# Two query-weight blocks kept in place of half a V tile, and the query block expanded by VectorE

## The chip, the core and the metric

One Trainium2 chip; the program runs on one core. The metric is device time in microseconds of one execution. The kernel before has a median of 177.51 us in three runs (177.19 to 177.63).

## What is computed

One token per sequence, four sequences, passes through two equal layers. Each layer adds attention over a cache (32 query heads, 8 key/value heads of 128, the last 2048 positions) and then a gated feed-forward block, each behind a normalisation.

```python
q = (x @ wq).reshape(B, Sq, Hq, Dh)            # x: 4 x 512, wq: 512 x 4096
k, v = k_cache[:, :, Sk - W:, :], v_cache[:, :, Sk - W:, :]
scores = einsum("bhqd,bhkd->bhqk", q, k) * Dh ** -0.5
o = einsum("bhqk,bhkd->bhqd", softmax(scores), v)
A(x) = o.reshape(B, Sq, Hq * Dh) @ wo
B(x) = (sigmoid(x @ w_gate) * (x @ w_up)) @ w_down
x = x + A(layernorm(x)); x = x + B(layernorm(x))   # twice, with the same weights and caches
```

## The kernel before

Nearly everything it does is stream weights and caches from HBM once per layer through 50 SBUF slots of 512 KB (`arena`) and one more buffer (`side`). K (16 MB) is read once and stays for both layers, transposed in place by VectorE (`k_transpose`, L887). V is read in both layers, except for what stays from the first to the second: tiles (7,1) and (6,1), tile (7,0), which is packed into PSUM in between, and half of tile (6,0). All these loads are issued by SyncE, in one fixed order, one call to `dma` (L401) each. A load waits until the slot it goes to has been released, and every load behind it waits too. `load` takes a slot pair from a pool in order of release; `load_half` names the half pair it will go to (`homes`), so its place and its releaser are written by hand.

The order of the instructions on each compute engine is made by a planner (`_schedule`) that runs when the program is built, from durations written down in the kernel. While the second layer is planned, `P.chain` fixes TensorE's order to that of the source; VectorE, ScalarE and GpSimdE are ordered by the planner.

The parts that the change touches:

- **Query weights of the second layer** (`load_wq`, L522 to 530; `q_mms`, L817; `q_second`, L857). wq is 512 x 4096, cut into four row blocks c of 128, each in two column halves i. Half i = 1 serves heads 4 to 7, which are attended first in the second layer (heads run 7 to 0). The piece (0,1) stays from the first layer (`keep_wq`, L632). Seven pieces of 512 KB are read again, in the order (1,1), (2,1), (3,1), (0,0), (1,0), (2,0), (3,0), where (c,i) names the row block and the half.
- **Half a V tile** (`keep_half`, L626; `load_v`, L609). The second half of V tile (6,0) stays, so the second layer reads only one half of that tile.
- **The query block** (`q_unit`, L867). For each head, four matmuls with a shifted window of a wide identity (L875) write a block-diagonal 128 x 256 query block into PSUM, and ScalarE copies it to SBUF (L880).
- **The score mask** (`e_m`, L902). Four matmuls of 32 output rows each (L905) put a large negative number into a score bank, before the sixteen score matmuls (L916) add to it.
- **The normalisation between feed-forward and second attention** (`layer_norm`, L743; end of `glu`, L1453). VectorE adds the feed-forward result to x (L1455), sums x (L754), TensorE sums over partitions (L759), and only then the query matmuls can start.

One head of attention in the second layer is called a unit here. In steady state, TensorE does per unit: value matmuls of this unit (L1088), a permutation of the next unit's probabilities (L957), the mask and scores of a unit three ahead (L905, L916), sums (L1064), the query block of the unit after that (L875), and an output projection (L1142). VectorE does: the row maximum of the scores (L929), a reciprocal (L1066), two half copies (L933), a masked maximum (L937, L941), a transposition and reduction of the value result (L1097, L1102, L1104), and the transposition of the probabilities (L964) for which the next value matmuls wait.

Of the kernel before, what the change touches and what calls it, by code (L numbers as in the profile page):

```python
# [7 lines left out]
BF16 = mybir.dt.bfloat16  # L8
ACTF = mybir.ActivationFunctionType
ALU = mybir.AluOpType  # L10
# [268 lines left out]
def build(nc, A_x, A_k, A_v, A_wq, A_wo, B_wg, B_wu, B_wd, out, cfg=None):  # L279
# [45 lines left out]
    with es:  # L325
        def sb(name, shape, dt):
            return es.enter_context(nc.sbuf_tensor(name, shape, dt))
# [10 lines left out]
        eyew = sb("eyew", [128, 224], BF16)  # L338
# [4 lines left out]
        msk_s = sb("msk_s", [128, 32], BF16)  # L343
# [76 lines left out]
        on_free = {}  # L420
        Y = ("V", HKV - 1, 0, 0)
        Z = ("V", HKV - 1, 1, 0)
        GA = ("V", HKV - 2, 0, 0)
        KEPT = ("kept",)
        WQ = ("wq", 0, 0)
        SP = ("side",)
# [11 lines left out]
        def take_load():  # L438
            take_k()
            assert can_take()  # L440
            name, emit = loads.pop(0)
            if name in homes:
                hfree.difference_update(home(name))
                s = home(name)[0]
            else:
                s = pool.alloc()
            where[name] = s
            if name in (Y, Z, GA, WQ):
                base[name] = s
            emit(s)  # L450
# [71 lines left out]
        def load_wq(k):  # L522
            if k == 0:
                for c in range(NC):
                    load(("wq", c, k), 2, "bw_8k", (2 * SLOT, wq_d[:, c, :], False))
            else:
                for i in (1, 0):
                    for c in range(i, NC):
                        load_half(("wq", c, k, i), wq_d[:, c, i * SLOT:(i + 1) * SLOT], "bw_4k", SLOT,
                                  (((Y, 0), (Y, 1), (WQ, 1), (WQ, 0)), (None, (WQ, 0), (GA, 0), (SP, 0)))[i][c])  # L530

# [22 lines left out]
        def load_glu(k):  # L554
            for nm, src, two in (("wg", wg_d, wg_p), ("wu", wu_d, wu_p)):
                if k == 0:
                    for c in range(NC):
                        load_half((nm, c, k), src[:, c, :], "bw_3k", F,
                                  (((WQ, 0), (GA, 0), (SP, 0), (Y, 0)), ((Y, 1), (Z, 0), (WQ, 0), (GA, 0)))[nm == "wu"][c])
                    continue  # L560
                for cc in range(NC // 2):
                    load((nm, cc, k), 2, "bw_8k", (2 * F, two[:, cc, :], False))
            for n, (a, b) in enumerate(bounds_of(k)):
                if k == 0:
                    load_half(("wd", a, k), wd_d[:, a:b, :].rearrange("p k n -> p (k n)"), "bw_4k", (b - a) * D,
                              ((SP, 0), (Y, 0), (Y, 1), (Z, 0))[n])
                else:
                    load(("wd", a, k), 1, "bw_8k", ((b - a) * D, wd_d[:, a:b, :], False))
# [40 lines left out]
        def load_v(h, bp, k, n_use):  # L609
            name = ("V", h, bp, k)  # L610
            tiles = {(HKV - 2, 0): ((GA, 0),), (HKV - 3, 1): ((Y, 0), (Y, 1))}.get((h, bp)) if k else None
            if tiles is not None:
                halves[h, bp] = []
                for n, tile in enumerate(tiles):
                    half = ("Vh", n, h, bp, k)
                    load_half(half, pair_d(A_v, h, bp)[:, :, n * SLOT:(n + 1) * SLOT], "bw_4k", SLOT, tile)
                    halves[h, bp].append((half, 0))
                if len(tiles) == 1:
                    halves[h, bp].append((KEPT, 0))
                return  # L620
            load(name, n_use, "bw_8k", (2 * SLOT, pair_d(A_v, h, bp), True))
# [4 lines left out]
        def keep_half(s):  # L626
            hfree.add(s)
            where[KEPT] = s + 1
            left[KEPT] = 2
        on_free[GA] = keep_half  # L630

        def keep_wq(s):  # L632
            hfree.add(s)
            name = ("wq", 0, 1, 1)
            where[name] = s + 1
            left[name] = 1
            on_free[name] = lambda s: hfree.add(s)
        on_free[WQ] = keep_wq

# [7 lines left out]
        P.op("gpsimd", "eyew0", 200.0, lambda g: g.memset(eyew[:], 0.0), w=[("eyew0",)])  # L647
# [4 lines left out]
        for jh in range(2):  # L652
            for bp in range(2):
                for i in range(2):
# [10 lines left out]
             lambda g: g.affine_select(msk_s[:, :].rearrange("p (i y) -> p i y", i=2),  # L665
                                       ones_f[:, :].rearrange("p (i y) -> p i y", i=2),
                                       [[1, 2], [0, NR]], ALU.is_equal, 0.0, base=-1, channel_multiplier=1),
# [15 lines left out]
             lambda v: v.tensor_reduce(eyew[:, 96:128], ident.rearrange("p (a j) -> p j a", a=4), AXX, ALU.max),  # L683
             r=[("e", 0), ("eyew0",)], w=[("eyew",)])
# [6 lines left out]
        ey = eyew[:, 96:128]  # L691
# [11 lines left out]
        P.op("vector", "selw", 100.0, lambda v: v.tensor_copy(selw[:, :], eyew[:, 96:96 + NB]), r=[("eyew",)], w=[("selw",)])  # L703
# [39 lines left out]
        def layer_norm(tag, b0, b1, for_q, add=None):  # L743
# [12 lines left out]
            if after is not None:  # L756
                after()
            P.op("tensor", "ln_sum" + tag, tm["pe_f32"],
                 lambda t: t.matmul(mean, ones_d, lnr[:, 0:nb], start=True, stop=True),  # L759
# [97 lines left out]
        def q_second(variance):  # L857
            q_mms(1, 1, WB, (0, 1))
            variance()
            unstash_half(tuple(named("ln_rd2Q")))  # L860
            q_mms(1, 1, WB, (2, 3))
            q_mms(1, 0, OBS[1], (0,))
            fresh.append(q_turn(1, 1, WB))
# [3 lines left out]
        def q_unit(tag, h, k2):  # L867
            hh = h % 4
            src = qh[32 * hh:32 * hh + 32, h // 4 * 64:h // 4 * 64 + 64].rearrange("p (x r) -> p x r", r=REP)
            dst = ps[:, CB, 0:256].rearrange("p (x y) -> p x y", y=NR)  # L870

            def e_qx(pe):
                last = None
                for a in range(4):
                    last = pe.matmul(dst[:, :, a * REP:(a + 1) * REP], eyew[32 * hh:32 * hh + 32, 96 - 32 * a:224 - 32 * a],  # L875
                                     src, start=True, stop=True)
                return last
            P.op("tensor", "qx" + tag, 250.0, e_qx, r=[("qh", h // 4), ("eyew",)], w=[("cb",)], banks=(CB,))
            P.op("scalar", "qe" + tag, c_act(256),
                 lambda a: a.copy(qbd[:, k2 * 256:(k2 + 1) * 256], ps[:, CB, 0:256]),  # L880
                 r=[("cb",)], w=[("q", k2)], banks=(CB,))
# [12 lines left out]
        def softmax_unit(tag, hk, wait=False, q=True, between=None):  # L894
# [7 lines left out]
            def e_m(pe):  # L902
                last = None
                for gi in range(4):
                    last = pe.matmul(ps[32 * gi:32 * gi + 32, bank, :], msk_s[:, :],  # L905
                                     msk_m[:, :].unsqueeze(1).broadcast_to([128, 256, 2]), start=True, stop=False)
                return last

            def e_s(pe):
                last = None if wait else e_m(pe)  # L910
                for cp in range(4):
                    for gi in range(4):
                        jh, bp = gi // 2, gi % 2
                        kt = kpair(hk, bp).rearrange("p (j c k t) -> p c t j k", c=2, k=32, t=2)
                        q0 = ((k2 * 4 + cp) * 2 + bp) * 32
                        last = pe.matmul(ps[32 * gi:32 * gi + 32, bank, :], qbd[:, q0:q0 + 32],  # L916
                                         kt[:, cp // 2, cp % 2, jh * NJ:(jh + 1) * NJ, :], start=False, stop=(cp == 3))
                return last
# [74 lines left out]
        def pv_unit(tag, h, k2, tiles, between=None):  # L993
            ob = OBS[k2]
            ev = ebuf[:, k2 * 256:(k2 + 1) * 256].bitcast(BF16).rearrange("p (m x t) -> p t m x", x=32, t=2)
            for n, (bp, name) in enumerate(tiles):
                if n and between is not None:
                    between()
                s = need(name)

                def e_pv(pe, s=s, bp=bp):
                    last = None
                    src = tile_ap(s)
                    for j in range(2 * NJ):
                        x0 = j // 16 * 16 + bp * 8
                        last = pe.matmul(ps[:, ob, bp * 8:bp * 8 + 8], src[:, j * 128:(j + 1) * 128],  # L1006
# [3 lines left out]
                     r=tok(s) + [("e", k2)], w=[("pso", k2, bp)], banks=(ob,))  # L1010
                done(name)
# [224 lines left out]
        def attn_second():  # L1236
# [33 lines left out]
            score(0, lambda: q_mms(1, 0, OBS[1], (1,)))  # L1270
            qx(1)
# [68 lines left out]
        def glu(k, b0, b1, add=None, last=False):  # L1340
# [29 lines left out]
            for n, nm in enumerate(("wg", "wu")):  # L1370
# [21 lines left out]
                if n == 0:  # L1392
# [11 lines left out]
                         lambda v: v.reciprocal(eg[:, 0:NH], eg[:, 0:NH]), r=[("eg",)], w=[("eg",)])  # L1404
            P.op("vector", "gh%d" % k, c_dve(NH),
# [30 lines left out]
            for (a, b) in bounds_of(k):  # L1436
# [3 lines left out]
                def e_d(pe, a=a, b=b, s=s):  # L1440
                    last = None
                    src = slot_ap(s)
                    for fc in range(a, b):
                        for c in range(NC):
# [8 lines left out]
            xts = [("xT", b) for b in range(b0, b1)]  # L1453
            P.op("vector", "gres%d" % k, tm["dve_fix"] + 40.0,
                 lambda v: v.tensor_tensor(bview(xT[:, 0:NX], b0, b1),  # L1455
                                           ps[:, CB, 128:128 + NC * nb].rearrange("p (c b) -> p c b", b=nb),
                                           bview(xT[:, 0:NX], b0, b1), ALU.add),
# [42 lines left out]
        q_second(layer_norm("Q", 0, NB, True))  # L1500
# [73 lines left out]
```

## Time and profile before

The profile is of one execution, which took 177.0 us; 175.3 us of it is the span from the first to the last instruction.

| | before |
|---|---|
| median of three runs | 177.51 us |
| profiled execution, span | 177.0 us, 175.3 us |
| read from HBM | 69.73 MB, mean 398 GB/s over the span |
| busy: TensorE, VectorE, ScalarE, GpSimdE | 105.7, 104.4, 32.7, 22.2 us |
| granted TensorE clock, mean | 0.949 |
| chain that ended last, by engine | DMA 52%, VectorE 24%, TensorE 19% |

How to read it: PE is TensorE's matmul row and PEld its weight loads, DVE is VectorE, ACT ScalarE, POOL GpSimdE, SP SyncE. A row such as `L929 DVE TENSOR_REDUCE small<-ps 128x1 f32<-128x512 f32 x16` names source line, engine, operation, the tile written and the tile read, shapes, and how many there were. In a timeline the first column is the start in us from the span's start, the second how long; square brackets tell how long the engine was idle before it and what ended that. A table by stages gives for each engine the busy time and the number of instructions, then granted clock, busy share of the DMA engines, and GB/s.

### The profile page before, as it was taken

Reading aid. Unit: us, or ns where it says so; the run is one execution under the profiler, and the core shown is the slowest. Engines: PE = TensorE matmul, PEld = TensorE weight load, DVE = VectorE, ACT = ScalarE, POOL = GpSimd, SP = SyncE. Lnnn points to the kernel's source line nnn. Section 1 sums busy time; section 2 is a strip of 40 time slices with the busy share of each in tenths; the row PEclk is TensorE's granted clock in tenths of the full one; section 3 lists DMA queues with packets and bytes.
Section 4 is the critical chain, followed back from the end, with each engine's and each line's share of the span. In section 5 each row is a group of like instructions: output and inputs, shape, how many; then the busy total and the mean of one; then the engine's idle time right before and its main releaser. Section 6 shows DMA issues by size and latency. Waiting matters only on the chain.

```text
span 175.3 us, 3927 instructions
## 1 busy us (share of the span) xinstructions
PE 105.7 (60%) x1661; PEld 54.7 (31%) x1661; DVE 104.4 (60%) x257; ACT 32.7 (19%) x87; POOL 22.2 (13%) x90
## 2 busy tenths in 40 slices
PE   0536246259566273661765456547977999776673
PEld 0203112014334041340445452142322444445321
DVE  6307997994957738378322381316299999751351
ACT  2002031322303003021030000100143455430011
POOL 6100010101101001010010000000011453442000
PEclk9999999999999999999999999999999999995555
DMA  5999999999999999999999999999999999999980
GB/s 188 426 426 426 426 419 424 408 421 423 419 419 412 420 424 426 421 405 427 419 419 415 415 400 407 402 410 403 394 413 404 423 419 424 421 416 423 419 344 25
DMA packets 12226, 70.00 MB, mean 399 GB/s; under 512 B 1320, under 2 KB 1328, under 8 KB 6064
## 3 DMA queue, kind: packets, MB, share of 16 engines
q1 hardware_dynamic: 12200, 69.74, 97.1%
q8 instruction: 13, 0.21, 0.5%
q14 instruction: 5, 0.04, 0.1%
q10 hardware_dynamic: 8, 0.00, 0.0%
HBM read 69.73 MB, written 0.00 MB: 398 GB/s over the span
## 4 chain that ended last, share of the span: by engine, by line
DMA 52%; DVE 24%; PE 19%; issue 2%; SPq 1%; ACT 0%; DVEq 0%
DMA arena<-in_A_v_cache_dram 20%; DMA arena<-in_B_w_down_dram 18%; DVE arena L887 12%; DMA arena<-in_A_wq_dram 10%; PE ps L916 8%; DMA arena<-in_B_w_gate_dram 5%; DVE small L929 3%; PE ps L905 3%; PE ps L1088 2%; DVE small L933 1%; DVE arena L593 1%; PE ps L1006 1%; DVE side L937 1%; PE ps L828 1%; DVE small L941 1%
## 5 line engine op out<-in xcount | busy, mean ns | idle before, releaser
L887 DVE STREAM_TRANSPOSE arena<-arena 128x1024 f32<-128x1024 f32 x32 | 37.0, 1205 | 0.1
L1006 PE MATMUL ps<-side,arena 128*128 128x8 bf16 x576 | 18.2, 168 | 14.1 <-DMA arena<-in_A_v_cache_dram 14.0
L916 PE MATMUL ps<-arena,side 128*32 128x512 bf16 x256 | 25.0, 524 | 0.1
L1006 PEld LDWEIGHTS ps<-side,arena 128*128 128x128 bf16 x576 | 16.7, 104 | 20.5 <-DMA arena<-in_A_v_cache_dram 18.8
L929 DVE TENSOR_REDUCE small<-ps 128x1 f32<-128x512 f32 x16 | 10.8, 676 | 17.6 <-PE ps L916 17.5
L944 ACT ACTIVATE side<-ps,small 128x512 bf16<-128x512 f32 x16 | 11.0, 687 | 36.8 <-PE ps L1024 18.3
L905 PE MATMUL ps<-small,msk_s 128*32 128x512 bf16 x64 | 8.4, 512 | 13.9 <-DVE arena L887 13.1
L880 ACT CAST side<-ps 128x256 bf16<-128x256 f32 x16 | 5.9, 370 | 34.4 <-PE ps L916 25.4
L959 ACT CAST side<-ps 128x512 bf16<-128x512 f32 x16 | 9.4, 586 | 10.8 <-PE ps L957 10.8
L916 PEld LDWEIGHTS ps<-arena,side 128*32 128x32 bf16 x256 | 8.2, 119 | 10.0 <-issue 7.2
L973 POOL CAST small<-small 128x1 bf16<-128x1 f32 x9 | 1.7, 188 | 76.1 <-ACT side L944 76.1
L957 PE MATMUL ps<-side,perm 128*128 128x512 bf16 x16 | 7.9, 494 | 5.2 <-ACT side L944 5.2
L828 PE MATMUL ps<-arena,xn 128*4 128x512 bf16 x60 | 7.5, 572 | 3.9 <-DMA arena<-in_A_wq_dram 3.6
L784 ACT ACTIVATE small<-ps 128x4 f32<-128x4 f32 x4 | 0.7, 174 | 48.1 <-PE ps L780 48.1
L1379 PE MATMUL ps<-arena,xn 128*4 128x448 bf16 x60 | 7.2, 549 | 3.3 <-DMA arena<-in_B_w_up_dram 1.5
L964 DVE STREAM_TRANSPOSE side<-side 128x256 f32<-128x256 f32 x16 | 6.9, 433 | 2.0 <-ACT side L959 1.8
L875 PE MATMUL ps<-side,eyew 32*128 32x64 bf16 x64 | 5.6, 217 | 3.4 <-ACT side L880 2.4
L1088 PE MATMUL ps<-arena,side 128*32 128x512 bf16 x112 | 7.3, 381 | 0.2 <-DVE small L941 0.2
L1014 DVE TENSOR_TENSOR onb<-ps,rinv 128x16 bf16<-128x16 f32 x9 | 1.7, 185 | 9.0 <-PE ps L1006 8.8
L905 PEld LDWEIGHTS ps<-small,msk_s 128*32 128x32 bf16 x64 | 1.7, 97 | 16.8 <-DVE arena L887 15.4
L1388 DVE STREAM_TRANSPOSE side<-ps 128x448 f32<-128x448 f32 x4 | 2.6, 650 | 7.3 <-PE ps L1379 7.3
L840 DVE STREAM_TRANSPOSE side<-ps 128x512 f32<-128x512 f32 x3 | 2.1, 716 | 7.9 <-PE ps L828 7.8
(123 smaller groups left out, 137.8 us busy)
## 6 DMA issues: line engine op xcount, KB each, us to landing
arena<-in_A_v_cache_dram SPq DMA_DIRECT2D x27, 1024.0 KB, 18.8
arena<-in_A_k_cache_dram SPq DMA_DIRECT2D x16, 1024.0 KB, 24.9
arena<-in_A_wq_dram SPq DMA_DIRECT2D x4, 1024.0 KB, 7.8
arena<-in_A_wo_dram SPq DMA_DIRECT2D x3, 1024.0 KB, 26.5
arena<-in_A_wq_dram SPq DMA_DIRECT2D x6, 512.0 KB, 6.3
arena<-in_B_w_up_dram SPq DMA_DIRECT2D x4, 448.0 KB, 6.1
arena<-in_B_w_gate_dram SPq DMA_DIRECT2D x2, 896.0 KB, 21.7
arena<-in_B_w_up_dram SPq DMA_DIRECT2D x2, 896.0 KB, 23.9
```

Of the source, the lines that this page charges most:

```text
L828: last = pe.matmul(ps[32 * hh:32 * hh + NB, qb, :], xn[:, c * NB:(c + 1) * NB], src[:, o + hh * 512:o + (hh + 1) * 512], start=(c == 0), s ...
L887: P.op("vector", "T%d_%d" % (h, t), c_dve(1024), lambda v, v32=v32: v.transpose(v32, v32), r=[("slot", 4 * h + t)], w=[("slot", 4 * h + t)])
L905: last = pe.matmul(ps[32 * gi:32 * gi + 32, bank, :], msk_s[:, :], msk_m[:, :].unsqueeze(1).broadcast_to([128, 256, 2]), start=True, stop= ...
L916: last = pe.matmul(ps[32 * gi:32 * gi + 32, bank, :], qbd[:, q0:q0 + 32], kt[:, cp // 2, cp % 2, jh * NJ:(jh + 1) * NJ, :], start=False, s ...
L929: lambda v: v.tensor_reduce(nmax[:, k2:k2 + 1], ps[:, bank, :], AXX, ALU.max),
L944: lambda a: a.activation(prow[:, :].rearrange("p (m x t) -> p m x t", x=32, t=2), ps[:, bank, :].rearrange("p (m t x) -> p m x t", x=32, t ...
L957: lambda pe: pe.matmul(ps[:, pb, :], perm[:, :], prow[:, :], start=True, stop=True),
L959: P.op("scalar", "pc" + tag, c_act(512), lambda a: a.copy(prow[:, :], ps[:, pb, :]), r=[("ppb", pb)], w=[("prow",)], banks=(pb,))
L964: P.op("vector", "pt" + tag, c_dve(256), lambda v: v.transpose(et, prow[:, :].bitcast(F32)), r=[("prow",)], w=[("e", k2)])
L1006: last = pe.matmul(ps[:, ob, bp * 8:bp * 8 + 8], src[:, j * 128:(j + 1) * 128], ev[:, j % 2, j % 16 // 2, x0:x0 + 8], start=(j == 0), stop ...
L1088: last = pe.matmul(ps[32 * g:32 * g + 32, ob, :], ew[:, g, mq, t], src.rearrange("p (m t d) -> p t m d", t=2, d=128)[:, t], start=(n == 0) ...
L1379: last = pe.matmul(ps[32 * g:32 * g + NB, gub[n], 0:NF], xn[:, c * NB:(c + 1) * NB], src[:, g * NF:(g + 1) * NF], start=(c == 0), stop=(c ...
```

## The change

- Of V tile (6,0) nothing stays any more; it is read in two halves in both layers, in the first layer into the two slots that the freed halves of the query weights left. The second layer reads one more half of a V tile.
- Of the query weights two pieces stay, (0,1) and (1,1). Six are read again, in the order (2,1), (0,0), (3,1), (1,0), (2,0), (3,0). Piece (0,0) thus comes ahead of (3,1). As before, ten half tiles are read around the second layer's queries, and as many bytes in the whole kernel.
- The pool loses a slot pair early, so most V and wo loads of the first layer wait for a release one later than before.
- The query block: one matmul with an identity repeated four times writes 128 x 64, and VectorE multiplies it by a mask into the 128 x 256 block. ScalarE's copy goes. In the second layer TensorE's order of the first two units changes a little: both query blocks and all the query matmuls of the pieces (0,0) and (1,0) now stand ahead of the first scores.
- The score mask is one matmul of 128 output rows.
- The sum over x is formed ahead of the feed-forward's end (`ln_rd0`) and put into PSUM by a matmul (`ln_old`); what is left to add behind the last feed-forward matmul is the sum of the feed-forward result, read straight from PSUM. The addition to x follows beside it.

The planner is run anew, so that VectorE's order changes: in the second layer, for the middle units, the masked maximum of a unit (L933, L937, L941) now follows the transposition of the probabilities of the unit before instead of standing around the value result's three instructions, and the new multiplication stands ahead of the row maximum.

```diff
-        msk_s = sb("msk_s", [128, 32], BF16)
+        msk_s = sb("msk_s", [128, 128], BF16)
...
-                for i in (1, 0):
-                    for c in range(i, NC):
-                        load_half(("wq", c, k, i), wq_d[:, c, i * SLOT:(i + 1) * SLOT], "bw_4k", SLOT,
-                                  (((Y, 0), (Y, 1), (WQ, 1), (WQ, 0)), (None, (WQ, 0), (GA, 0), (SP, 0)))[i][c])
+                for c, i, place in ((2, 1, (WQ, 0)), (0, 0, (WR, 0)), (3, 1, (SP, 0)), (1, 0, (Y, 0)), (2, 0, (Y, 1)), (3, 0, (WQ, 1))):
+                    load_half(("wq", c, k, i), wq_d[:, c, i * SLOT:(i + 1) * SLOT], "bw_4k", SLOT, place)
...
-            tiles = {(HKV - 2, 0): ((GA, 0),), (HKV - 3, 1): ((Y, 0), (Y, 1))}.get((h, bp)) if k else None
+            tiles = ({(HKV - 2, 0): ((WR, 1), (WQ, 0)), (HKV - 3, 1): ((WR, 0), (Y, 0))} if k
+                     else {(HKV - 2, 0): ((WQ, 0), (WR, 0))}).get((h, bp))
...
-        on_free[WQ] = keep_wq
+        on_free[WQ], on_free[WR] = keep_wq(0), keep_wq(1)
...
+        P.op("vector", "eye4", 150.0,
+             lambda v: v.tensor_copy(eye4[:, 32:128].rearrange("p (a j) -> p a j", j=32),
+                                     eye4[:, 0:32].unsqueeze(1).broadcast_to([128, 3, 32])),
+             r=[("eyew",)], w=[("eye4",)])
...
-            def e_qx(pe):
-                last = None
-                for a in range(4):
-                    last = pe.matmul(dst[:, :, a * REP:(a + 1) * REP], eyew[32 * hh:32 * hh + 32, 96 - 32 * a:224 - 32 * a],
-                                     src, start=True, stop=True)
-                return last
-            P.op("tensor", "qx" + tag, 250.0, e_qx, r=[("qh", h // 4), ("eyew",)], w=[("cb",)], banks=(CB,))
-            P.op("scalar", "qe" + tag, c_act(256),
-                 lambda a: a.copy(qbd[:, k2 * 256:(k2 + 1) * 256], ps[:, CB, 0:256]),
+            P.op("tensor", "qx" + tag, 150.0,
+                 lambda pe: pe.matmul(dst, eye4[32 * hh:32 * hh + 32, :], src, start=True, stop=True),
+                 r=[("qh", h // 4), ("eye4",)], w=[("cb",)], banks=(CB,))
+            P.op("vector", "qe" + tag, c_dve(256),
+                 lambda v: v.tensor_tensor(
+                     qbd[:, k2 * 256:(k2 + 1) * 256].rearrange("p (x a r) -> p x a r", a=4, r=REP),
+                     dst.rearrange("p (x r) -> p x r", r=REP).unsqueeze(2).broadcast_to([128, NR, 4, REP]),
+                     maskp[:, :].unsqueeze(1).unsqueeze(3).broadcast_to([128, NR, 4, REP]), ALU.mult),
...
-                for gi in range(4):
-                    last = pe.matmul(ps[32 * gi:32 * gi + 32, bank, :], msk_s[:, :],
-                                     msk_m[:, :].unsqueeze(1).broadcast_to([128, 256, 2]), start=True, stop=False)
+                return pe.matmul(ps[:, bank, :], msk_s[:, :],
+                                 msk_m[:, :].unsqueeze(1).broadcast_to([128, 256, 2]),
+                                 start=True, stop=False, skip_group_check=True)
...
-            score(0, lambda: q_mms(1, 0, OBS[1], (1,)))
-            qx(1)
+            score(0, lambda: qx(1))
...
+            if not last:
+                P.op("vector", "ln_rd0", tm["dve_small"],
+                     lambda v: v.tensor_reduce(nmax[:, 0:NB], xT[:, 0:NX].rearrange("p (n b) -> p b n", b=NB), AXX, ALU.add),
...
+                if a == 0:
+                    P.op("tensor", "ln_old", tm["pe_f32"],
+                         lambda t: t.matmul(ps[:, CB, 192:192 + nb], inv_d[:, 0:1].broadcast_to([128, 128]), nmax[:, 0:nb],
+                                            start=False, stop=False, skip_group_check=True),
...
-        q_second(layer_norm("Q", 0, NB, True))
+        q_second(layer_norm("Q", 0, NB, True, (ps[:, CB, 128:128 + NX], [("cb",)], (CB,), x_add)))
```

## The prediction, made before the changed kernel ran

> **What bounds the kernel now.** I read the page's slices first. The DMA row stands at 9 from the second slice almost to the end, and the rate hardly leaves 400 to 426 GB/s: the kernel is a stream of 69.73 MB, and no compute change can end it before that stream ends.
>
> ```profile
> DMA  5999999999999999999999999999999999999980
> GB/s 188 426 426 426 426 419 424 408 421 423 419 419 412 420 424 426 421 405 427 419 419 415 415 400 407 402 410 403 394 413 404 423 419 424 421 416 423 419 344 25
> ```
>
> Then the question is whether compute reaches the end together with the stream. A table by stages answers for the second layer's attention (126.6 to 150), its tail, and the rest:
>
> ```profile
> 126.60:150.00 23.40, 20.95 (x298) 8.81 (x297) 21.84 (x68) 10.58 (x29) 7.60 (x23) 1.00 1.01 417
> 150.00:157.57 7.57, 5.25 (x85) 3.25 (x82) 4.50 (x15) 3.67 (x9) 3.77 (x12) 1.00 1.00 415
> 157.57:168.00 10.43, 7.26 (x135) 4.64 (x131) 3.24 (x15) 0.77 (x5) 0.91 (x2) 0.50 1.02 422
> ```
>
> In 126.6 to 150 VectorE is busy 21.84 of 23.40 us, and the view of its waits has a single one there, 3.2 us ending at the first row maximum (126.62). The timeline of VectorE for one unit shows what that means:
>
> ```profile
> 143.28 0.65 DVE L929 TENSOR_REDUCE small<-ps 128x1 f32<-128x512 f32 x1
> 143.85 0.18 DVE L1066 RECIPROCAL arena<-ps 64x8 f32<-64x8 f32 x1
> 144.06 0.33 DVE L933 COPY small<-small 64x1 f32<-64x1 f32 x2
> 144.43 0.25 DVE L937 SCALAR_TENSOR_TENSOR side<-small,maskr 128x32 f32<-128x32 f32 x1
> 144.72 0.21 DVE L941 TRANSPOSE_TENSOR_REDUCE small<-side 128x1 f32<-128x32 f32 x1
> 144.85 0.67 DVE L1097 STREAM_TRANSPOSE arena<-ps 128x512 f32<-128x512 f32 x1
> 145.56 0.44 DVE L1102 TENSOR_REDUCE arena<-arena 128x32 f32<-128x128 f32 x1
> 146.03 0.18 DVE L1104 COPY arena<-arena 64x32 f32<-64x32 f32 x1
> 146.24 0.45 DVE L964 STREAM_TRANSPOSE side<-side 128x256 f32<-128x256 f32 x1
> 146.61 0.65 DVE L929 TENSOR_REDUCE small<-ps 128x1 f32<-128x512 f32 x1
> ```
>
> Each instruction starts at most 0.04 us behind the end of the one ahead, and 0.08 us before it where it doesn't need it and that one is long (143.85, 144.85, 146.61). VectorE never stands still: a unit is 3.33 us (143.28 to 146.61) because VectorE's ten instructions fill it. TensorE's rows are packed too, but its value matmuls (L1088) start at 143.50 and 146.83, each 0.14 us behind the end of VectorE's transposition (143.36 and 146.69); they follow VectorE. Last, the timeline of the end:
>
> ```profile
> 168.14 0.10 PEld L1379 LDWEIGHTS ps<-arena,xn 128*4 128x4 bf16 x8 [0.95 <-DMA arena<-in_B_w_up_dram]
> ...
> 169.79 0.22 DVE L1406 TENSOR_TENSOR rinv<-side,onp 128x56 bf16<-128x56 f32 x1
> 170.64 0.73 PEld L1420 LDWEIGHTS ps<-arena,rinv 128*4 128x4 bf16 x32 [1.65 <-DMA arena<-in_B_w_down_dram]
> ...
> 171.86 0.31 PEld L1420 LDWEIGHTS ps<-arena,rinv 128*4 128x4 bf16 x16 [0.49 <-DMA arena<-in_B_w_down_dram]
> ...
> 172.48 0.10 PEld L1420 LDWEIGHTS ps<-arena,rinv 128*4 128x4 bf16 x8 [0.32 <-DMA arena<-in_B_w_down_dram]
> ```
>
> The stream ends the kernel, but the compute chain is close behind. **Its slack** is: about 0.1 us at the last w_up tile (matmuls before it done near 168.06, go on at 168.16); 0.57 at the first w_down tile (h ready at 170.01, 0.05 to signal, start 170.64); 0.2 at the second (171.66 to 171.86); nothing at the third. Together 0.9 us. And from 126.6 to 170 this chain has hardly another wait: PE's value matmuls of the next-to-last head start at 155.61, those of the last head's second tile at 160.10, neither marked as waiting for DMA (the last head's first tile, at 156.92, waits 0.2 for one, beside that chain).
>
> **The change, part by part.**
>
> *VectorE's new multiplication* (128x256, from PSUM, times a mask) is the term that counts: sixteen times one VectorE instruction in place of ScalarE's copy (L880, 0.37 each). No row has it. The nearest rows are of L1014 (16 elements, mean 185 ns), L1029 (64 elements from PSUM times the same mask, 225 ns) and L929 (512 elements from PSUM, 676 ns). From the last two, 256 elements lie at 225 + 192 x (676 - 225)/448 = 418 ns. Next to instructions that don't need it, it occupies 0.42 - 0.08 = 0.34 us. Bounds: below, 0.15 (as cheap as L1029's 64 elements, overlapped); above, 0.48 (as L964's 0.45, no overlap, 0.03 behind it); the middle rests on the two rows around it.
>
> Of the second layer's eight, two stand before the first row maximum, where VectorE waits 3.2 us anyway; cover gone, 0.34 each. The other six stand in the packed stretch: 6 x 0.34 = 2.04 us. The new order of VectorE's instructions saves nothing: the same ones stand in a unit, and I sum 3.69 us for it where 3.33 stood.
>
> *An earlier start of the second layer.* The third piece read, (3,1), still ends the wait for the first query half (matmuls 121.65, one after the other to 122.25). But piece (1,0), which was the fifth and held the first scores up (matmuls at 124.25, scores at 124.64), is now the fourth and comes when the fourth came (matmuls at 122.96). Then: 122.96 + 0.56 to the query block's matmul, about 0.3 until it is read, 0.42 for VectorE, 0.1 for signals and the second block's matmul: scores at 124.35, 0.3 earlier. Bounds 0 and 0.6.
>
> *Mean summed ahead*: the addition (L1455, 0.17, and the 0.04 behind it) leaves the way to the first query matmul. That saves 0.2 us at 119.66, and the wait for piece (3,1) takes it back; without that wait it would be worth 0.2. `ln_rd0` and `ln_old` lie in waits of VectorE and TensorE for other matmuls and for w_down tiles (1.1 us at L1445).
>
> *Mask and query block on TensorE*: one full-width matmul of 512 columns takes 0.32 us from start to start (L957) where the four narrow ones take 0.23 (144.93 to 145.16); one query matmul instead of four takes perhaps 0.1 where four take 0.22. The sum is near zero, from -0.12 to +0.12 per unit, and VectorE hides it; if TensorE were the bound it would be that, six times.
>
> *First layer*: eight more multiplications and `eye4`, 2.7 us and 0.2, on a VectorE that is full up to about 57 us. They are hidden behind loads: value matmuls wait 14.0 us for V tiles (L1006), and a V tile lands 18.8 us (median) behind its issue. The loads now issued one release later, up to about 4 us late (V (5,1): 76.1 in place of 72.9), and those behind them in SP's queue use that depth. If it ran out, each us late would be one more at the end. The added half tile is paid for by the query piece; reading V (6,0) as two halves costs 1.05 MB at 402 in place of 417 GB/s (stages with and without half tiles), 0.09 us of the stream.
>
> **The sum**: 2.04 - 0.30 = 1.74 us later at h; the slack takes 0.9; 0.8 remains. On the profiled execution 177.0 + 0.8 = 177.8. That execution lies 0.5 below the median of the runs, 177.51; on the median it is **178.3**.
>
> The copies at L933 and L1104 don't overlap what follows them (0.03 behind their ends); the rows from 512 elements down to the reciprocal's do. The Trainium skill, "VectorE: DVE Perf Modes", section "The DRAIN you can't avoid", says that the next instruction does not start until the pipeline is empty. By that rule, nothing would overlap, which the trace contradicts at 143.85 (L1066 starts 0.08 before L929 ends). It is a rival for the new instruction alone.
>
> **The rivals.**
>
> 1. *Hidden*: the stream ends last after all. It decides once the six cost less than 0.9 + 0.3 = 1.2 us, 0.20 each, near the lower bound, or if the first scores come 0.8 us earlier. For it: ScalarE loses its copies, and the masked maximum no longer cuts into the value result's instructions. Against it: VectorE's packed rows. 177.51 + 0.09 = 177.6, no change.
> 2. *Not overlapped*: the multiplication behaves like the half copies and holds what follows. 6 x (0.42 + 0.03) = 2.7; less 0.3 and 0.9 it is 1.5: 179.0.
> 3. *Faster*: the stream itself ends sooner. The DMA engines do not finish together: their share is 0.92 in 168 to 170 and 0.35 in 170 to 172. That is 0.08 x 2 + 0.65 x 2 = 1.5 us of idleness; were it halved, the last tile would land up to 0.7 us sooner, if compute followed: 176.8. Nothing in the change aims at it, and compute has no such reserve.
> 4. *The queue runs dry* at 116 to 126, where a query piece lands some 6 us behind its issue and takes 1.25 us: a release over 2 us late stalls the stream. The releasers keep their places, so I see no cause: 179.5.
> 5. *TensorE stays at full clock longer.* It was granted 1.00 up to 157.57 and 0.50 from there; the sixteen gate matmuls (L1379, 164.97) take 1.66 us. At full clock they would take half, and 0.8 is what was lost: 177.5. The Trainium skill, "TensorE: Matmul & The Clock Gate", "Part 1", has the clock fall after an idle window of about 3.4 us; attention ending later would move that by a window, but three would be needed to reach 164.97.
>
> **How the numbers follow.** Chances: forecast 0.50, hidden 0.27, not overlapped 0.08, faster 0.07, queue dry 0.03, clock 0.05. A measurement of this kernel can tell about 0.3% (0.5 us) from no change. Faster is rival 3: 0.07; same is rivals 1 and 5: 0.32; slower the rest: 0.61. The range goes from the hidden case, less the runs' own 0.3, 177.3, to the upper bound of the multiplication, 6 x 0.48 - 0.3 - 0.9 = 1.7, and 0.1 for a later start, 179.3.
>
> **What would show it.** Right: VectorE without waits in the second layer's attention, a unit near 3.7 us, the new line at 0.4 us; the gate matmuls, L1420's first ones 1.0 to 1.8 us later, L1420 waiting for VectorE and no longer for w_down. Wrong: a unit still near 3.3 us, or L1420's three waits for DMA as before (hidden); a DMA share under 1.0 before 168 (queue dry); an earlier last landing (faster).

## The result, and the profile after

The changed kernel takes 178.50 us (median of 11 runs, 177.86 to 180.52) where the kernel before takes 177.51 (11 runs on the same chip, 176.97 to 178.45): a ratio of 1.0067, 95% interval 1.0044 to 1.0091. A second series gave 178.80 (7 runs) and 177.19 (24 runs), ratio 1.0083 (1.0046 to 1.0120). So it is slower, by 1.0 to 1.6 us; 178.3 was forecast. The profiled execution took 178.32 us, span 176.5.

First the page's slices of the changed kernel, the rows for DMA and for its rate:

```profile
DMA  5999999999999999999999999999999999999970
GB/s 175 427 434 416 423 425 427 411 413 420 423 433 405 421 420 414 420 413 428 418 411 420 408 401 403 402 412 371 388 382 427 425 420 420 420 419 422 417 320 4
```

The stream still never pauses. It dips to 371 to 388 GB/s around 120 to 130 us and lands its last tile at 173.01 instead of 172.44. Next the table by stages, the same stretches as before:

```profile
126.60:150.00 23.40, 20.13 (x237) 7.35 (x233) 21.84 (x68) 8.02 (x21) 7.30 (x21) 1.00 1.01 414
150.00:157.57 7.57, 4.61 (x56) 2.53 (x55) 5.74 (x17) 3.13 (x8) 2.80 (x7) 1.00 1.01 418
157.57:168.00 10.43, 7.08 (x158) 5.26 (x162) 3.58 (x15) 1.21 (x5) 2.19 (x9) 0.58 1.02 420
```

VectorE is busy just as long up to 150 (21.84 us, 68 instructions), but it has got less far: in 150 to 157.57, where it had 4.50 us to do, it now has 5.74. Now VectorE's timeline of the changed kernel, from the unit of 4.10 us into the one behind it:

```profile
147.19 0.45 DVE L958 STREAM_TRANSPOSE side<-side 128x256 f32<-128x256 f32 x1
147.67 0.15 DVE L927 COPY small<-small 64x1 f32<-64x1 f32 x1
147.85 0.43 DVE L931 SCALAR_TENSOR_TENSOR side<-small,maskr 128x32 f32<-128x32 f32 x1
148.32 0.21 DVE L935 TRANSPOSE_TENSOR_REDUCE small<-side 128x1 f32<-128x32 f32 x1
...
149.13 0.36 DVE L872 TENSOR_TENSOR side<-ps,small 128x256 bf16<-128x256 f32 x1
149.53 0.33 DVE L927 COPY small<-small 64x1 f32<-64x1 f32 x2
...
151.29 0.45 DVE L958 STREAM_TRANSPOSE side<-side 128x256 f32<-128x256 f32 x1
151.66 0.72 DVE L931 SCALAR_TENSOR_TENSOR side<-small,maskr 128x32 f32<-128x32 f32 x1
152.42 0.21 DVE L935 TRANSPOSE_TENSOR_REDUCE small<-side 128x1 f32<-128x32 f32 x1
```

The new line (L872) is there, at 0.36 us. The surprise is L931, the masked maximum: 0.43 and 0.72 us, where it took 0.25 in every unit of the stretch before. GpSimd's timeline of the same kernel shows what else ran:

```profile
147.57 0.67 POOL L1105 TENSOR_TENSOR arena<-arena 64x256 bf16<-64x256 f32 x1
...
151.67 0.66 POOL L1105 TENSOR_TENSOR arena<-arena 64x256 bf16<-64x256 f32 x1
```

Both times L931 ends 0.04 to 0.05 us behind the end of GpSimd's product (148.28 against 148.24, 152.38 against 152.33). In the kernel before, the product lay beside the row maximum (143.28) and was over when the masked maximum started (L937, 144.43, shown in the prediction):

```profile
143.28 0.67 POOL L1109 TENSOR_TENSOR arena<-arena 64x256 bf16<-64x256 f32 x1
```

From one probabilities' transposition to the next the units are 3.60, 3.61, 3.79 and 4.10 us (136.19, 139.79, 143.40, 147.19, 151.29), and 5.29 to the next one; they were 3.33 to 3.38, and 4.40. Last the end, TensorE's matmuls:

```profile
171.13 0.64 PE L1358 MATMUL ps<-side,xT 128*4 128x128 f32 x8
172.44 1.66 PE L1419 MATMUL ps<-arena,rinv 128*4 128x128 bf16 x56 [0.67 <-DVE rinv L1405]
```

All 56 w_down matmuls run in one go and wait for VectorE's h; the three waits for w_down tiles are gone. Compute now ends last, as forecast.

### The profile page after: what moved, and what is told of

The parts are those of the page before. It is cut to its first block, busy times and chain, and to the rows that moved or that the text cites. A ratio compares the mean times of both kernels' runs of the same rounds, so it can differ in the third digit from the quotient of the medians.

```text
span 176.5 us, 3748 instructions
## 1 busy us (share of the span) xinstructions
PE 106.1 (60%) x1567; PEld 52.9 (30%) x1567; DVE 110.2 (62%) x275; ACT 27.3 (15%) x71; POOL 22.0 (12%) x89
## 4 chain that ended last, share of the span: by engine, by line
DMA 40%; DVE 27%; PE 18%; SPq 8%; issue 3%; ACT 1%; POOL 1%; POOLq 0%; DVEq 0%
DMA arena<-in_A_v_cache_dram 33%; SPq L401 8%; DVE arena L882 5%; PE ps L1001 4%; PE ps L909 4%; DMA arena<-in_A_wq_dram 4%; DMA arena<-in_B_w_up_dram 3%; DVE small L923 3%; DVE arena L1093 3%; PE ps L1374 2%; DVE side L958 2%; DVE arena L1098 2%; DVE side L931 2%; DVE arena L591 1%; PE ps L898 1%
## 5 line engine op out<-in xcount | busy, mean ns | idle before, releaser
L909 PE MATMUL ps<-arena,side 128*32 128x512 bf16 x256 | 25.5, 534 | 0.2 <-DVE side L872 0.2
L898 PE MATMUL ps<-small,msk_s 128*128 128x512 bf16 x16 | 8.4, 523 | 14.0 <-DVE arena L882 10.3
L909 PEld LDWEIGHTS ps<-arena,side 128*32 128x32 bf16 x256 | 6.4, 114 | 12.9 <-issue 10.3
L1084 PE MATMUL ps<-arena,side 128*32 128x512 bf16 x112 | 7.3, 380 | 0.0
L872 DVE TENSOR_TENSOR side<-ps,small 128x256 bf16<-128x256 f32 x16 | 6.1, 383 | 0.9 <-PE ps L869 0.9
L898 PEld LDWEIGHTS ps<-small,msk_s 128*128 128x128 bf16 x16 | 1.6, 101 | 16.6 <-DVE arena L882 11.0
L576 DVE STREAM_TRANSPOSE ps<-arena 128x512 f32<-128x512 f32 x4 | 2.8, 716 | 5.2 <-DMA arena<-in_A_v_cache_dram 5.1
```

The lines of the kernel that those rows point to most:

```text
L898: return pe.matmul(ps[:, bank, :], msk_s[:, :], msk_m[:, :].unsqueeze(1).broadcast_to([128, 256, 2]), start=True, stop=False, skip_group_c ...
```

## The experiments

A yardstick for all of them is the **path**: from the start of the first row maximum to the start of the last head's transposition of probabilities (126.62 and 156.33 in the kernel before). It repeats to some 0.1 us between traces of one kernel (29.71 and 29.75 before, 32.10 and 32.16 changed), and to 0.2 where the last head waits for a V tile. In block_only and block_mask it also holds the waits that are told below, and is no measure of VectorE's work alone.

| kernel | path, us | masked maximum at its longest, us | median, us | ratio to before (95%) |
|---|---|---|---|---|
| before | 29.71 | 0.25 | 177.2 to 177.5 | |
| loads_only | 29.75 | 0.25 | 177.97 | 1.0045 (1.0027 to 1.0063) |
| loads_mean | 29.94 | 0.25 | 177.76 | 1.0021 (1.0001 to 1.0042) |
| mean_only | 29.73 | 0.26 | 177.05 | 0.9995 (0.9975 to 1.0014) |
| on_scalar | 29.60 | 0.25 | 177.73 | 1.0010 (0.9986 to 1.0034) |
| mask_late | 31.14 | 0.28 | 177.69 | 1.0023 (1.0005 to 1.0040) |
| changed | 32.10 | 0.72 | 178.50 | 1.0067 (1.0044 to 1.0091) |
| mask_order | 32.12 | 0.25 | 178.04 | 1.0044 (1.0014 to 1.0074) |
| block_early | 32.24 | 0.72 | 179.26 | 1.0116 (1.0066 to 1.0167) |
| twice | 34.71 | 0.26 | 181.02 | 1.0188 (1.0141 to 1.0234) |
| block_only | 35.29 | 0.72 | 182.34 | 1.0286 (1.0241 to 1.0332) |
| block_mask | 37.38 | 0.72 | 182.55 | 1.0287 (1.0254 to 1.0320) |

(The masked maximum is that of the first seven heads; the eighth's is 0.25 to 0.30 everywhere. Where it is 0.72, that is the seventh head's, and the sixth's is 0.43 or 0.44.)

### Parts alone: the loads, the mean

loads_only takes the tiles that stay, their places and the order of the pieces from the change, with the matmuls and V tiles that follow from them, and nothing else; loads_mean adds the mean; mean_only has the mean alone; before_again is the kernel before, unedited. In all of them the query block and the mask stay as before. The edits' cores:

```diff
# loads_only, loads_mean
+                for c, i, place in ((2, 1, (WQ, 0)), (0, 0, (WR, 0)), (3, 1, (SP, 0)), (1, 0, (Y, 0)), (2, 0, (Y, 1)), (3, 0, (WQ, 1))):
...
+            score(0, lambda: qx(1))
# loads_mean, mean_only
+                 lambda t: t.matmul(mean, ones_d, lnr[:, 0:nb], start=tag != "Q", stop=True, skip_group_check=tag == "Q"),
```

> The tiles that stay and the order of the query pieces alone, on the kernel before. Theory 1: 177.5 to 177.6 us (0.09 us for the two half tiles). First scores up to 0.3 us earlier than in the kernel before, taken back by the stream. Rival (loads): 178.0 to 178.5. Beside the run with the mean summed ahead it shows what that edit is worth: by the prediction 0 (the wait for piece (3,1) takes its 0.2 us back).

> The changed kernel without its query block and score mask edits: only the tiles that stay, the order of the query pieces and the mean summed ahead. Theory 1: 177.5 us, within 0.3 (stream plus 0.09; the first scores earlier by up to 0.3, hidden by the stream at the end), units of 3.33 us, three waits for w_down as before. Rival (loads): 178.0 to 178.5, with the last landing 0.5 us or more later than in the kernel before and compute waiting for it.

> The mean summed ahead alone, on the kernel before. The prediction: 0.2 us saved on the way to the first query matmul and taken back by the wait for piece (3,1), the stream ending last: 177.4 us, within 0.3 of the kernel before. Rival (it makes the kernel faster): 177.1 us or less.

> The kernel before once more, for a second trace of its stream. If the stream's lag of 0.4 to 0.7 us at 120 to 134 us in the traces with the changed loads comes from the loads, this one shows at most 0.2 us of lag behind the first trace there. If it is the scatter of single executions, it may lag by 0.4 us too.

The mean alone changes nothing: 0.9995. In its trace the sum's matmuls on TensorE start 0.82 us behind the start of the last w_down matmuls, where 0.96 stood before; the first scores are no earlier for it, and the stream ends last, as forecast. The two kernels with the new loads are slower by 0.2 to 0.45%, 0.4 to 0.8 us, more than the 0.09 forecast. That is less than the changed kernel's loss for loads_mean; for loads_only the two intervals overlap. In loads_mean the stream ends last, with three waits as before:

```profile
171.59 0.74 PEld L1419 LDWEIGHTS ps<-arena,rinv 128*4 128x4 bf16 x32 [1.24 <-DMA arena<-in_B_w_down_dram]
172.83 0.31 PEld L1419 LDWEIGHTS ps<-arena,rinv 128*4 128x4 bf16 x16 [0.51 <-DMA arena<-in_B_w_down_dram]
173.47 0.10 PEld L1419 LDWEIGHTS ps<-arena,rinv 128*4 128x4 bf16 x8 [0.33 <-DMA arena<-in_B_w_down_dram]
```

Why the loads cost that much stays open. By the packets of the traces the new loads are 0.4 to 1.0 us behind the kernel before's first trace at 132 us, but before_again (177.9 us, one run) is 0.65 behind there too, and mean_only 0.41. Single traces scatter by as much as the effect.

### The query block alone

```diff
# block_only: the query block's lines of the change; block_mask: and the mask's
+                 lambda pe: pe.matmul(dst, eye4[32 * hh:32 * hh + 32, :], src, start=True, stop=True),
...
+            P.op("vector", "qe" + tag, c_dve(256),
# block_early: block_only, and of the change also
-            q_mms(1, 0, OBS[1], (0,))
+            q_mms(1, 0, OBS[1], (0, 1))
...
-            score(0, lambda: q_mms(1, 0, OBS[1], (1,)))
-            qx(1)
+            score(0, lambda: qx(1))
```

> The kernel before, with the query block's part of the change alone (one matmul on 32-fold repeated columns and VectorE's multiplication by the mask, instead of four matmuls and ScalarE's copy). Theory 1 (VectorE's multiplication carries the loss): six multiplications of 0.36 us in the packed stretch and 0.6 us of the masked maximum's stretching beside GpSimd make 2.7 us; 0.9 is slack; without the earlier first scores 1.2 to 1.8 us are left, so 178.7 to 179.3 us beside 177.5 of the kernel before, a unit of 3.6 us or more from value transposition to value matmuls, and the last w_down matmuls waiting for VectorE. Rival (the loss comes from the loads, whose last one landed 0.57 us later): 177.5 us, within 0.3.

> The query block's part and the one-matmul score mask, on the kernel before. The prediction costs the mask at -0.12 to +0.12 us per unit on TensorE, hidden by VectorE: so the time of the query block alone, within 0.2 us. If TensorE follows as closely as VectorE, six units of up to 0.1 us show: 0.3 to 0.6 us from it, either way.

> The query block's part on the kernel before, as in the run with that part alone, and now with the second block made ahead of the first scores' end, where the change has it; the loads stay as before. Theory 1: of the 5.0 us of the run with the block alone, 3.7 were the second scores' wait for VectorE's multiplication behind four stash transpositions; that wait goes, and the price of the multiplications in the packed stretch stays: 178.2 to 178.9 us. Rival (the block itself costs 5 us where the loads are not changed): 181 to 182.5 us.

block_only missed both expectations: 182.34 us, 5 us slower than before. Its TensorE and then VectorE show why:

```profile
126.43 0.23 PE L875 MATMUL ps<-side,eye 32*128 32x64 bf16 x1
126.59 0.62 PE L906 MATMUL ps<-small,msk_s 128*32 128x512 bf16 x4
130.89 1.90 PE L917 MATMUL ps<-arena,side 128*32 128x512 bf16 x16 [3.69 <-DVE side L878]
```

```profile
128.06 2.46 DVE L593 STREAM_TRANSPOSE arena<-ps 128x512 f32<-128x512 f32 x4
130.45 0.39 DVE L878 TENSOR_TENSOR side<-ps,small 128x256 bf16<-128x256 f32 x1
```

The second head's block is ready for VectorE at 126.6, but stands behind the first softmax and four transpositions of the stashed V tile in VectorE's order. ScalarE's copy, on an idle engine, never had that queue. The second scores wait 3.69 us. The loads that go to the second head's K slots wait with them, and the stream falls to 216 GB/s in that slice of the page: here the queue did run dry. Both blocks ahead of the first scores, which the change brings in another part of the diff, is what avoids this. block_early shows it: the wait goes, 179.26 us. That is 0.4 above the range I gave, because with the old order of the pieces the second block waits for the fifth piece: first scores at 125.72, 0.83 later than in the changed kernel. block_mask took 182.55 us: beside block_only the single mask matmul makes no difference that can be seen in the times. The two traces can't be compared: in block_mask's, TensorE was granted half the clock from 130.4 to 137.3 us and from 157.7 to 161.1, and its rows there are slower than block_only's (sixteen score matmuls take 1.90 us, from 135.04, against 1.17, from 134.66).

### The multiplication on another engine, and twice

on_scalar is the changed kernel with the mask product on ScalarE; twice repeats it on VectorE in the second layer.

```diff
# on_scalar
+                for i in range(4):
+                    last = a.activation(dq[:, :, i], dst.rearrange("p (x r) -> p x r", r=REP), ACTF.Copy,
+                                        scale=maskp[:, i:i + 1])
# twice
-            P.op("vector", "qe" + tag, c_dve(256),
+            for qe in ("qe", "qd")[:1 + (tag[0] == "2")]:
+                P.op("vector", qe + tag, c_dve(256) / 2 ** (tag[0] == "2"),
```

> The changed kernel with the mask product on ScalarE: four copies of 64 elements with a scale for each partition in place of VectorE's one multiplication; the one query matmul, the wide score mask, the loads and the mean stay as changed. Theory 1: VectorE's multiplication carries the loss, so this is the run without the block again, 177.8 us within 0.3, the stream ending last, units near 3.35 us. Rival (TensorE's wide mask and single query matmul carry it): 178.5 us as the changed kernel.

> The changed kernel with VectorE's multiplication of each query block done twice in the second layer (the second writes the same values again). Theory 1: VectorE is the bound from the first row maximum on and the slack at the end is used up, so six more of 0.33 to 0.36 us come out whole: 2.0 to 2.2 us more, 180.5 to 180.7 us, and units 0.36 us longer. Rival (hidden behind the stream or TensorE): 178.5 to 179.0 us.

on_scalar is back at 177.73 us with units of 3.28 to 3.35 and L931 at 0.25, although TensorE's new mask and single query matmul are still there. ScalarE needs 0.92 us for its four copies, in time that it had. So what the changed kernel loses beyond its loads comes with VectorE's multiplication and the order that goes with it. twice is 2.2 to 2.5 us above the changed kernel, a little over the expectation, and not by the reason given: the two multiplications take 0.82 us where one takes 0.36, so a unit is 4.07 to 4.11 us, 0.48 over mask_late's. In its order the masked maximum starts 0.2 us before GpSimd's product ends, as in mask_late, and keeps its 0.25. Its path also holds a wait of 0.66 us for TensorE (at 134.26), which was at half the clock from 132.3 to 135.7 us.

### The order of the masked maximum

```diff
# mask_order (ahead of the call of the planner)
+        for u in range(NW - 1):
+            by["tv2.%d" % u].deps.add(by["nx12.%d" % (u + 2)])
+            by["pt2.%d" % (u + 1)].deps.add(by["mk2.%d" % (u + 2)])
# mask_late (there too)
+        for u in range(NW - 2):
+            by["nx02.%d" % (u + 2)].deps.add(by["pt2.%d" % (u + 1)])
+            by["nx12.%d" % (u + 2)].deps.add(by["pt2.%d" % (u + 1)])
```

> The changed kernel with VectorE's masked maximum back between the value result's copy and the probabilities' transposition, its place in the kernel before (two dependencies a unit, no work added or left out). Theory 1a: the masked maximum's stretching from 0.25 to 0.72 us beside GpSimd's product is on the path, 0.6 us in all; it goes, and 178.5 becomes 177.9 us (the run without the block, 177.8, is the floor). Theory 1b: the multiplications alone carry the loss, and the order of a unit is worth nothing: 178.5 us, within 0.3.

> The changed kernel once more, beside the next run on the same chip: 178.5 us within 0.4, its masked maximum stretched to 0.43 and 0.72 us in the fourth and fifth unit as before (both come from the order, not from chance), units 3.60, 3.60, 3.8, 4.1.

> The changed kernel with the order of its first three units kept in the fourth and fifth: the masked maximum's two copies wait for the probabilities' transposition there too, so that the masked maximum no longer falls beside GpSimd's product. No work added or left out. If the stretching beside GpSimd is a price of its own: no masked maximum over 0.3 us, all four units 3.60 to 3.65, the value matmuls 0.6 to 0.7 us earlier than in the changed kernel, 177.8 to 177.9 us beside 178.5 (the stream's floor with these loads is 177.7). Rival (the order only moves the time, as in the run with the masked maximum ahead, whose units were all 3.75): 178.3 to 178.5 us, units 3.75.

mask_order takes the stretching away and gains nothing on the path (32.12): with the masked maximum ahead, every unit is 3.74 to 3.79. Its time, 178.04 us, can't be told from the changed kernel's, and TensorE's clock may have a part in it: in its trace full clock came back at 171.69 us, and the w_down matmuls took 0.95 us instead of the changed kernel's 1.66. Of its 12 runs, the three with a mean granted clock of 0.952 took 179.20 to 179.35 us, the nine with 0.958 or more 177.39 to 178.41; no run held the clock fixed. It was therefore not the test that I took it for: it changed two things at once.

after_again stretches L931 to 0.43 and 0.72 in the same two places: the order decides it, not chance. block_only, block_mask and block_early show the same two stretches (0.43 or 0.44, and 0.72), and there too the masked maximum ends 0.04 to 0.06 us behind the product. mask_late keeps the good order of the first three units. Its VectorE, and GpSimd beside it, in the unit that was 4.10 us:

```profile
147.37 0.45 DVE L958 STREAM_TRANSPOSE side<-side 128x256 f32<-128x256 f32 x1
147.85 0.33 DVE L927 COPY small<-small 64x1 f32<-64x1 f32 x2
148.21 0.25 DVE L931 SCALAR_TENSOR_TENSOR side<-small,maskr 128x32 f32<-128x32 f32 x1
...
148.71 0.36 DVE L872 TENSOR_TENSOR side<-ps,small 128x256 bf16<-128x256 f32 x1
149.00 0.67 DVE L923 TENSOR_REDUCE small<-ps 128x1 f32<-128x512 f32 x1
...
150.98 0.45 DVE L958 STREAM_TRANSPOSE side<-side 128x256 f32<-128x256 f32 x1
```

```profile
147.74 0.67 POOL L1105 TENSOR_TENSOR arena<-arena 64x256 bf16<-64x256 f32 x1
```

The two copies now fill the time of the product and are not slowed by it; L931 starts 0.20 before the product ends and keeps its 0.25. The reciprocal of the sums (L1062), which the changed kernel has behind the row maximum in these units, stands ahead of it again, so mask_late moves more than L931. Units are 3.61 to 3.62, the path 31.14. The time is 177.69 us beside 178.80 of the changed kernel in the same series; the intervals do not overlap. At its end the stream and compute are about level. The weight loads wait for the stream, by 0.22 us at the last eight:

```profile
171.81 1.19 PEld L1419 LDWEIGHTS ps<-arena,rinv 128*4 128x4 bf16 x48 [1.14 <-DMA arena<-in_B_w_down_dram]
173.22 0.10 PEld L1419 LDWEIGHTS ps<-arena,rinv 128*4 128x4 bf16 x8 [0.22 <-DMA arena<-in_B_w_down_dram]
```

The matmuls themselves still start 0.15 us behind h and run in one go, as in the changed kernel:

```profile
171.84 1.68 PE L1419 MATMUL ps<-arena,rinv 128*4 128x128 bf16 x56 [0.67 <-DVE rinv L1405]
```

So mask_late and on_scalar both beat the changed kernel by about 1 us. Neither beats the kernel before. on_scalar stops where its stream ends (three waits for w_down tiles, as in loads_mean); mask_late comes out at the same 177.7 with, in its trace, compute just ending last.

## Why the prediction came out right, step by step

The direction and the size were right, the size partly by luck, because errors cancel. Against the forecast sum the multiplications cost 0.6 us less, the order of VectorE's instructions 1.0 more, the first scores came 0.5 later than forecast, and the slack was 0.5 larger: 0.4 us more in all.

- **VectorE bounds the second layer, and compute ends last**: right. The timeline marks no wait of VectorE between the first row maximum (126.84) and 155.21, and L1419 waits for L1405. The signs that were named for the case of being right came, but the gate matmuls were 2.6 us later, not 1.0 to 1.8. One reading of the unit was off: of the three overlaps of 0.08 us, that at 144.85 follows an instruction of 0.21 us, so a long instruction ahead is not the condition.
- **The multiplication, 0.42 long, 0.34 occupied, 2.04 in all**: its length is 0.36 to 0.38 (interpolated 0.42), and the row maximum starts 0.29 behind its start (149.00 against 148.71). Without the stretching the six cost 31.14 - 29.72 = 1.42 us of path, 0.24 each: between the bounds of 0.15 and 0.48, but 0.6 us less than the value taken. The sum of 3.69 for a unit is 3.61.
- **"The new order of VectorE's instructions saves nothing"**: this step failed. The order is worth something both ways. With copies and masked maximum behind the transposition a unit is 3.61 where mask_order's is 3.75. But the planner keeps that order for three units only, and what it does in the later ones costs 32.10 - 31.14 = 1.0 us of path. By the rows L931's two stretches are 0.18 and 0.47 long, 0.65 together, but they did not arrive one for one: three of the last intervals between transpositions are 0.17, 0.49 and 0.32 us longer than mask_late's (3.79, 4.10 and 5.29 against 3.62, 3.61 and 4.97). The first of these has no stretch in it, and the last, which has the 0.47, ends in both kernels behind a wait of VectorE for the value matmuls (1.00 and 0.71 us). The stretches and the rest of the order were not tried apart. What the order loses besides is overlap: with a half copy behind it the multiplication holds 0.40 us (149.13 to 149.53) and not 0.29, and a row maximum 0.71 (145.03 to 145.74) and not 0.60. The prediction added up VectorE's durations for one unit, and never laid GpSimd's timeline beside them.
- **First scores 0.3 earlier**: they came at 124.89, 0.25 later. The steps from the fourth piece's matmuls to the scores took 1.43 us where 1.39 was reckoned; the piece itself landed at 123.41 and not at 122.92; 0.3 of those 0.49 us the whole trace was late already, as the piece ahead of it shows (121.89 after 121.60). In the kernels with the new loads the first row maximum starts at 126.5 to 127.3, in those with the old loads and ScalarE's copy at 126.6 to 127.0: no gain.
- **Slack of 0.9 us**: it is 1.4. The 2.6 us by which path and start are later (gate matmuls at 167.57 after 164.97) arrive as 1.2 at the last matmuls. 0.32 stood in the second w_up matmuls (1.98 us, now 1.66) where I took 0.1; 0.49 ahead of the first w_down matmuls (0.57 taken); and 0.57 inside the w_down matmuls (2.23 us from first to last, now 1.66) where I took 0.2.
- **The sum**: 1.74 - 0.9 = 0.8 was forecast; 2.6 - 1.4 = 1.2 it is by the spans of the two profiled executions (176.5 and 175.3).
- **Mask and query matmul near zero**: right; on_scalar has both and units of 3.33. **Mean worth nothing**: right. **First layer hidden**: right as far as seen; the bytes landed by 110 us are 0.25 us behind, 0.18 of it already at 10 us.
- **The loads' 0.09 us**: too low. Three kernels whose stream ends last have the new loads (loads_only, loads_mean, on_scalar), at 1.0010 to 1.0045; that is 0.2 to 0.8 us. The cause stays open.

Of the rivals, *hidden* is nearly what the multiplication alone does: its 1.42 us are about the slack, and mask_late can't be told from on_scalar. What shows in the changed kernel is the 1.0 us of the later units' order. *Not overlapped* falls where the row maximum follows (0.29 us), and holds where a half copy does (0.40); the section that I drew on for it, in the Trainium skill's "VectorE: DVE Perf Modes", also says that a next instruction which is not held starts earlier, and that is what the 0.29 us show. *Faster* falls: the last tile landed 0.57 us later. *TensorE at full clock longer* falls in this execution: full clock lasted to 159.18 instead of 157.57, and the gate matmuls still took 1.66 us. (Its 1.00 up to 157.57 holds, by the matmuls' rows, only from about 127 us; the last section says why.) *Queue runs dry* did not occur here; block_only shows that it is near.

That L931 is stretched by a conflict over SBUF between the two engines is an explanation that no run isolated: mask_late moved the instruction, and no run changed only what GpSimd reads. The Trainium skill, "SBUF — State Buffer", section "Who interferes with whom", says that a VectorE instruction with two SBUF inputs contends with a GpSimd instruction that reads SBUF, that such contention is an exclusive lock, and that issue order decides which of the two blocks. L931 reads `small` and `maskr`, and it ends 0.04 to 0.05 us behind L1105 both times; the two half copies, with one input each, run beside it in mask_late at their usual 0.33 for both. In two points the trace differs or says more. At 151.66 L931's record starts 0.01 us ahead of L1105's, and it waited all the same. And only 0.04 to 0.05 us of L931 lie behind the product's end, not its whole 0.25; in mask_late too it ends 0.05 behind (148.46 against 148.41) without having been stretched.

## What to carry to other kernels

Before an instruction is moved on a packed engine, lay the other engines' timelines beside its new place; a short instruction can grow to three times its length beside another engine's with which it shares no data. When work goes from an idle engine to a full one, its price is not only its duration but also the queue that it joins: 3.7 us for one multiplication of 0.4 in block_only. And slack at the end is best measured from the busy groups themselves (how much longer they take than without waits), not from the waits marked in front of them.

## What the runs showed of the hardware that was not expected

VectorE's masked maximum of 32 elements took up to 0.72 us instead of 0.25 beside GpSimd's product of 256. A packet of 4 KB takes 0.16 us in the median, but single ones took up to 1.28 us in the changed kernel's first trace. There 78 of 2816 took over one and a half times the median, in its second trace (after_again) 31; in the two traces of the kernel before it was 20 and 31 of 2560. Nearly all of them lie between 118 and 130 us. So two traces of one kernel differ as much as the two kernels do, and what makes these packets long, no run shows.

And the page's granted clock can mislead. For the profiled execution of mean_only it shows half the clock from about 48 to 129 us, for that of the kernel before full clock there. But the matmuls of the two take equally long, as these query matmuls show, the first line of the kernel before, the second of mean_only:

```profile
119.66 1.02 PE L828 MATMUL ps<-arena,xn 128*4 128x512 bf16 x8 [0.26 <-DVE xn L762]
```

```profile
119.73 1.02 PE L828 MATMUL ps<-arena,xn 128*4 128x512 bf16 x8 [0.27 <-DVE xn L762]
```

A 512-column matmul of L957 takes 0.594 us in the mean between 60 and 126 us in both executions, and 0.390 between 130 and 150 us in both. The trace of the kernel before holds no record of the clock ahead of 126.85 us, so the 1.00 that the page gives for that time, and with it the mean of 0.949, is not borne out by its rows. The two executions took 177.0 and 177.12 us.
